# Chunk attention and a gated feed-forward on one core: q and k loaded as 4 KB runs over all partitions, with block 0 in eight PSUM banks and a moved schedule for block 3

## The chip, the core and the metric

The kernel runs on one core of a Trainium2 chip. The metric is the device time of one execution in microseconds. TensorE (PE) does the matmuls, VectorE (DVE), ScalarE (ACT) and GpSimd (Pool) the rest; SyncE (SP) and ACT issue the DMAs, which all run on the core's 16 DMA engines.

## The reference, cut

```python
# q, k, v: (8, 8, 576, 64) fp32: batch, heads, tokens, head_dim.  Attention inside chunks of 64 tokens.
scores = 1/8 * q_c @ k_c.T ;  attn = softmax(scores) ;  out = attn @ v_c
x = out.transpose(0, 2, 1, 3).reshape(4608, 512)          # tokens x (heads * head_dim)
h = x @ w_in                                              # 512 -> 2048
y = (h * 1/(1 + exp(-beta * h))) @ w_out                  # 2048 -> 512
```

## The kernel before

The 4608 tokens are cut into nine blocks of 512, that is of eight chunks. A batch element has nine chunks, so blocks 1 to 7 cross from one element to the next, and their q and k come in two pieces: 1 and 7 chunks in block 1, then 2 and 6, 3 and 5, 4 and 4, and so on. Blocks 0 and 8 come in one.

For each block, q and k are loaded, cast to bf16, transposed (blocks 0 to 2 on PE, with copies out of PSUM by ACT and DVE; the others by a DMA transpose, with "order copies" on Pool), and the attention runs in the four PSUM banks of A. Its result is xT, the moving operand of the first matmul (mm1); tanh on ACT and a product on DVE give g, and the second matmul (mm2) makes the output. mm1 of one block and mm2 of the one before it alternate on PE, and the attention of the next block is threaded between them. Order within each engine's queue comes from a list of events with a time each: `at(time, function, ...)`. One unit of that time is one matmul group of PE.

Some names: PSUM is the memory that PE writes its results to, here eight banks, four called A and four F. "Order copies" put the transposed tokens back in their order (qkO). R holds the reciprocals of the softmax sums, Rhi and Rs are made from it, and "spread" is the matmul that brings Rs to all tokens. The clock granted to PE stands in the trace as full or half; PEclk is its mean in a stretch.

```python
        def load_qk(blk, which, h0, n_h, queue):              # q: partitions 0-63, k: 64-127
            s, src = blk % NQS, (q, k)[which]
            for b, c, n, at in chunk_runs(blk):
                def f(e, b=b, c=c, n=n, at=at):
                    a = src[b][h0:h0 + n_h, 64 * c:64 * (c + n), :]
                    r = 64 * which + 8 * at
                    return e.dma_start(qkstage[r:r + 8 * n, s, h0:h0 + n_h, :],
                                       a.rearrange("h (p i) d -> p h (i d)", i=8))
                P.dma(queue, f, ...)
        ...
        def order_qk(blk, hp, eng):
            copy_cast(eng, in_order(hp), qkT[:, :, hp, :].rearrange("k i t -> k t i"), ...)
        ...
        attention(0, -45, 1)
        at(12, load_qk, 1, 0, 0, 8, "sp")
        at(15.9, load_qk, 1, 1, 0, 8, "act")
        at(12.1, load_v, 1)
        ...
        for blk in range(3, NB):
            t0, u = base(blk - 1) + 1.5, 1
            if blk == 3:
                t0, u = base(2) + 4, 0.85
            loads = 30.5 if blk == 3 else t0 - 24
            ...
            for hp in range(4):
                at(40.5 if blk == 3 else t0 - 16.9, cast_qk, blk, hp, "pool")
                at(t0 - 6.5 + 1.25 * hp, order_qk, blk, hp, "pool")
            ...
            at(41 if blk == 3 else t0 - 15.5, transpose_dma, blk)
            attention(blk, t0, u)
```

The softmax here doesn't subtract the row's maximum and nothing guards it: scores larger than these inputs give would overflow.

Of the kernel before, what the change touches and what calls it, by code (L numbers as in the profile page):

```python
# [7 lines left out]
F32 = dt.float32  # L8
# [3 lines left out]
def K(*key, v=0):  # L12

    return key, v
# [143 lines left out]
def bass_chunk_attention__then__act_swish_beta_kernel(nc, q, k, v, w_in, w_out, beta, out):  # L158
# [8 lines left out]
    with ExitStack() as es:  # L167
# [17 lines left out]
        qkstage = sb("qkstage", [128, NQS, H, 512], F32)  # L185
        vstage = sb("vstage", [128, NVS, 4, H, 64], F32)
        qkcast = sb("qkcast", [128, 8, H, 64], BF16)
        qkT = sb("qkT", [128, 8, 4, 128], BF16)
        qkO = sb("qkO", [128, 4, 2, 8, 64], BF16)
# [70 lines left out]
        def load_qk(blk, which, h0, n_h, queue):  # L260
            s, src = blk % NQS, (q, k)[which]
            for b, c, n, at in chunk_runs(blk):
                def f(e, b=b, c=c, n=n, at=at):
                    a = src[b][h0:h0 + n_h, 64 * c:64 * (c + n), :]
                    r = 64 * which + 8 * at
                    return e.dma_start(qkstage[r:r + 8 * n, s, h0:h0 + n_h, :],
                                       a.rearrange("h (p i) d -> p h (i d)", i=8))
                P.dma(queue, f, writes=[K("qkstage", s, hp, which, at, v=blk)
                                        for hp in range(h0 // 2, (h0 + n_h) // 2)])
# [56 lines left out]
        def cast_qk(blk, hp, eng):  # L326
            s = blk % NQS
            dst = qkcast[:, :, 2 * hp:2 * hp + 2, :].rearrange("p i h d -> p h i d")
            src = qkstage[:, s, 2 * hp:2 * hp + 2, :].rearrange("p h (i d) -> p h i d", i=8)
            keys = [K("qkstage", s, hp, which, at, v=blk)  # L330
                    for which in range(2) for _, _, _, at in chunk_runs(blk)]
            if eng == "act":
                P.op("act", lambda e: e.activation(dst, src, AF.Copy),
                     reads=keys, writes=[K("qkcast", hp, v=blk)])
            else:
                P.op(eng, lambda e: e.tensor_copy(dst, src),  # L336
                     reads=keys, writes=[K("qkcast", hp, v=blk)])

        def transpose_dma(blk):
            P.dma("sp", lambda e: e.dma_start_transpose(  # L340
                qkT[:, :, :, :].rearrange("p i h t -> p (i h) t"),
                qkcast[:, :, :, :].rearrange("p i h d -> p (i h d)")),
                reads=[K("qkcast", hp, v=blk) for hp in range(4)],
                writes=[K("qkT", hp, v=blk) for hp in range(4)])

# [6 lines left out]
        def in_order(hp):  # L352
            return qkO[:, hp, :, :, :].rearrange("k w c (p i) -> k (w c p) i", i=8)

        def order_qk(blk, hp, eng):
            copy_cast(eng, in_order(hp), qkT[:, :, hp, :].rearrange("k i t -> k t i"),
                      [K("qkT", hp, v=blk)], [K("qkO", hp, v=blk)])

        def transpose_pe(blk, hp, ps, psname, eng):
            dst = ps[:, hp, :].bitcast(BF16).rearrange("p (i t) -> p i t", i=8)  # L360
            for i in range(8):
                P.op("pe", lambda e, i=i: e.transpose(  # L362
                    dst[:, i, :], qkcast[:, i, 2 * hp:2 * hp + 2, :].rearrange("p h d -> p (h d)"),
                    identity[:, :]),
                    reads=[K("qkcast", hp, v=blk), K("identity")],
                    writes=[K(psname, hp, v=("t", blk))])
            copy_cast(eng, in_order(hp), dst.rearrange("k i t -> k t i"),
# [249 lines left out]
```

## Time and profile before

Median 362.75 us of 3 runs (361.68 to 363.59); the profiled run has a span of 361.4 us.

| Stage of the profiled run, us | What PE waits for |
|---|---|
| 0 to 27.8 | start-up: loads, then the attention of block 0 |
| 27.8 to 43.3 | nothing: mm1 of block 0 |
| 43.3 to 58.9 | k of block 1 |
| 58.9 to 79.1 | the attention of block 1, step by step |
| 79.1 to 116.8 | blocks 1 and 2 side by side: gaps of 0.2 to 2.4 us, 7 us in all, most for steps of block 2's attention |
| 116.8 to 127.75 | the fourth order copy of block 3 |
| 128.5 to the end | nothing: 32.6 us per block |

The windows view of the kernel before gives the busy time of each engine in four of these stretches. The columns are named in its first line; "(x193)" is the number of instructions.

```profile
core 0: us, PE busy (x) PEld busy (x) DVE busy (x) ACT busy (x) POOL busy (x), PEclk, DMA share, GB/s
0.00:27.80 27.80, 10.42 (x193) 7.53 (x194) 11.03 (x28) 9.13 (x13) 8.08 (x18) 1.00 1.03 259
43.30:58.90 15.60, 8.58 (x36) 3.31 (x36) 1.43 (x3) 2.00 (x4) 3.00 (x5) 0.96 1.03 184
116.80:128.50 11.70, 0.43 (x16) 0.43 (x18) 0.00 (x0) 0.00 (x0) 6.64 (x7) 0.60 0.90 167
189.80:222.40 32.60, 31.29 (x292) 15.35 (x300) 14.84 (x23) 17.28 (x28) 13.83 (x12) 1.00 0.93 188
```

In the steady stretch (the last line) PE is busy 31.29 of 32.60 us. In the stretch before block 1 it is busy 8.58 of 15.60, in the one before block 3's last scores 0.43 of 11.70.

The timeline of the kernel before, around block 1. Columns: start, duration, engine, line and operation, and in brackets the idle time before it with what ended it.

```profile
42.66 0.91 ACTq L266 DMA_DIRECT2D qkstage<-in_k_dram  x2
...
58.15 2.14 DVE L336 CAST qkcast<-qkstage 128x1024 bf16<-128x1024 f32 x2 [14.09 <-DMA qkstage<-in_k_dram]
...
58.91 2.74 PE L362 MATMUL A<-identity,qkcast 128*128 128x128 bf16 x24 [5.34 <-DVE qkcast L336]
```

The load of k is issued by ACT only at 42.66 us, behind the last tanh of block 0. DVE sits idle 14.09 us until it has landed, and PE 5.34 us more after its last filler.

The timeline of the kernel before, around the scores of block 3 (qkO is their operand, written by the order copies).

```profile
116.42 0.32 PE L383 MATMUL A<-qkO 64*64 64x64 bf16 x16 [0.57 <-POOL qkO L350]
121.86 3.99 POOL L336 CAST qkcast<-qkstage 128x1024 bf16<-128x1024 f32 x4 [5.50 <-DMA qkstage<-in_k_dram]
125.80 1.90 POOL L350 COPY qkO<-qkT 128x1024 bf16<-128x1024 bf16 x1
...
127.75 0.43 PE L383 MATMUL A<-qkO 64*64 64x64 bf16 x16 [11.02 <-POOL qkO L350]
```

The first three of the four order copies are done by 116.4 us. The fourth (125.80) stands in Pool's queue behind the four casts of block 4 (121.86), and these wait for block 4's k. So PE waits 11.02 us for a copy whose data had been there all along.

The DMA view of the kernel before in two windows: 20 to 27 us, where only w_in is loaded, and 112 to 121 us, where mostly q and k of block 4 are. "Share" is the time that the packets took, as a share of 16 engines' time.

```profile
DMA packets 1353, 2.70 MB, mean 386 GB/s; under 512 B 42, under 2 KB 42, under 8 KB 1352
q1 hardware_dynamic: 1352, 2.68, 103.8%
...
DMA packets 1459, 1.79 MB, mean 199 GB/s; under 512 B 660, under 2 KB 660, under 8 KB 1459
q1 hardware_dynamic: 1459, 1.79, 108.3%
```

The engines are busy in both, but move 386 GB/s in the one and 199 in the other.

### The profile page before, as it was taken

The numbers are of one execution on the slowest core, as the hardware profiler recorded it, in microseconds if no ns is written. First come the engines' busy times: TensorE is split into PE (matmuls) and PEld (weight loads), VectorE is DVE, ScalarE is ACT, GpSimd is POOL, SyncE is SP. The second block draws the span as 40 slices with busy tenths as digits, with TensorE's granted clock in tenths as the row PEclk, the third lists the DMA queues.
The fourth block names the chain that finished last, engine by engine and source line by source line (L and its number), as shares of the span: only waits on it lengthen the run. The fifth ranks groups of instructions, "written<-read, shape, count | busy, mean of one in ns | idle before, by whom it ended". The sixth has DMA issues, their size and how long they took to land.

```text
span 361.4 us, 6228 instructions
## 1 busy us (share of the span) xinstructions
PE 301.7 (83%) x2646; PEld 148.1 (41%) x2688; DVE 148.2 (41%) x234; ACT 165.5 (46%) x262; POOL 115.2 (32%) x126
## 2 busy tenths in 40 slices
PE   0559974598768089999899999999999999999996
PEld 0433423345323034454445445444544444444442
DVE  3445703238444015533653453355344535534400
ACT  1355613427633035546455553655465455554421
POOL 0347524015046549128244643920630000000000
PEclk9999996869969569999999999999999999999999
DMA  8998999998779978899999979981011000001012
GB/s 149 229 387 310 273 165 215 156 186 187 134 143 210 202 134 167 191 172 143 176 212 200 184 170 221 235 146 48 31 44 44 31 29 32 29 34 55 29 60 87
DMA packets 83517, 52.85 MB, mean 146 GB/s; under 512 B 65569, under 2 KB 65569, under 8 KB 83489
## 3 DMA queue, kind: packets, MB, share of 16 engines
q1 hardware_dynamic: 74586, 39.85, 56.0%
q10 hardware_dynamic: 8902, 12.59, 13.1%
q8 instruction: 21, 0.34, 0.4%
q14 instruction: 8, 0.06, 0.1%
HBM read 36.71 MB, written 9.44 MB: 128 GB/s over the span
## 4 chain that ended last, share of the span: by engine, by line
PE 70%; DMA 9%; DVE 6%; ACT 6%; issue 3%; POOL 3%; SPq 2%; ACTq 0%; DVEq 0%; POOLq 0%
PE F L452 31%; PE F L468 28%; DMA qkstage<-in_k_dram 9%; PE A L416 3%; ACT tt L458 3%; PE A L383 3%; ACT E L389 2%; POOL qkcast L336 2%; DVE R L402 2%; PE A L429 2%; PE A L362 1%; SPq L340 1%; DVE g L461 1%; PE A L395 1%; DVE Rs L406 1%
## 5 line engine op out<-in xcount | busy, mean ns | idle before, releaser
L461 DVE SCALAR_TENSOR_TENSOR g<-tt,F 128x512 bf16<-128x512 bf16 x144 | 99.0, 687 | 152.7 <-ACT tt L458 152.7
L458 ACT ACTIVATE tt<-F,beta_half 128x512 bf16<-128x512 f32 x144 | 98.9, 687 | 123.2 <-PE F L452 123.2
L452 PE MATMUL F<-xT,w_in_bf 128*128 128x512 bf16 x552 | 146.0, 390 | 3.5 <-issue 1.6
L468 PE MATMUL F<-w_out_bf,g 128*128 128x512 bf16 x558 | 144.4, 386 | 4.5 <-POOL w_out_bf L322 1.7
L468 PEld LDWEIGHTS F<-w_out_bf,g 128*128 128x128 bf16 x576 | 55.4, 99 | 68.3 <-issue 3.5
L452 PEld LDWEIGHTS F<-xT,w_in_bf 128*128 128x128 bf16 x576 | 55.5, 100 | 67.9 <-issue 5.5
L350 POOL COPY qkO<-qkT 128x1024 bf16<-128x1024 bf16 x24 | 45.7, 1945 | 59.0 <-PE A L383 29.7
L336 POOL CAST qkcast<-qkstage 128x1024 bf16<-128x1024 f32 x30 | 30.5, 1057 | 73.0 <-DMA qkstage<-in_k_dram 59.8
L473 ACT ACTIVATE ostage<-F 128x512 f32<-128x512 f32 x36 | 21.5, 597 | 28.0 <-PE F L468 28.0
L436 ACT ACTIVATE o_sb<-A 128x512 f32<-128x512 f32 x36 | 20.9, 594 | 16.6 <-PE F L468 5.5
L441 DVE TENSOR_TENSOR xT<-o_sb,A 128x512 bf16<-128x512 f32 x36 | 24.1, 681 | 6.7 <-PE A L416 6.7
L389 ACT ACTIVATE E<-A 128x512 bf16<-128x512 f32 x36 | 20.7, 595 | 7.7 <-PE A L383 5.2
L350 POOL CAST v_bf<-vstage 128x512 bf16<-128x512 f32 x36 | 21.4, 630 | 5.2 <-DMA vstage<-in_v_dram 5.2
L383 PE MATMUL A<-qkO 64*64 64x64 bf16 x576 | 11.4, 201 | 13.8 <-POOL qkO L350 11.6
L416 PE MATMUL A<-Rs,sel 128*128 128x128 bf16 x144 | 13.4, 243 | 10.7 <-DVE Rs L406 7.1
L416 PEld LDWEIGHTS A<-Rs,sel 128*128 128x128 bf16 x144 | 10.3, 110 | 17.6 <-DVE Rs L406 11.2
L383 PEld LDWEIGHTS A<-qkO 64*64 64x64 bf16 x576 | 9.8, 114 | 17.7 <-POOL qkO L350 11.8
L362 PE MATMUL F<-identity,qkcast 128*128 128x128 bf16 x32 | 4.1, 310 | 12.9 <-DVE qkcast L336 10.9
L402 DVE RECIPROCAL R<-A 128x128 f32<-128x128 f32 x9 | 8.6, 952 | 8.4 <-PE A L395 8.4
L322 POOL CAST w_out_bf<-wstage 128x512 bf16<-128x512 f32 x16 | 9.1, 613 | 7.3 <-DMA wstage<-in_moe_w_out_dram 7.3
L336 DVE CAST qkcast<-qkstage 128x1024 bf16<-128x1024 f32 x4 | 3.8, 970 | 16.8 <-DMA qkstage<-in_k_dram 16.8
L362 PE MATMUL A<-identity,qkcast 128*128 128x128 bf16 x64 | 6.2, 266 | 5.3 <-DVE qkcast L336 5.3
(29 smaller groups left out, 66.8 us busy)
## 6 DMA issues: line engine op xcount, KB each, us to landing
out_dram<-ostage ACTq DMA_DIRECT2D x36, 256.0 KB, 3.4
vstage<-in_v_dram SPq DMA_DIRECT2D x32, 256.0 KB, 11.9
wstage<-in_moe_w_in_dram SPq DMA_DIRECT2D x4, 1024.0 KB, 10.2
wstage<-in_moe_w_out_dram SPq DMA_DIRECT2D x4, 1024.0 KB, 9.5
qkstage<-in_q_dram SPq DMA_DIRECT2D x2, 896.0 KB
qkstage<-in_q_dram SPq DMA_DIRECT2D x6, 256.0 KB, 6.4
qkstage<-in_q_dram SPq DMA_DIRECT2D x2, 768.0 KB, 10.7
qkstage<-in_k_dram ACTq DMA_DIRECT2D x5, 256.0 KB, 8.5
```

What stands on the lines that cost most here:

```text
L336: P.op(eng, lambda e: e.tensor_copy(dst, src), reads=keys, writes=[K("qkcast", hp, v=blk)])
L350: P.op(eng, lambda e: e.tensor_copy(dst, src), reads, writes)
L383: return e.matmul(A[64 * g:64 * g + 64, 2 * u + hb, col:col + 64], qkO[r, hp, 1, 2 * cc + g, :], qkO[r, hp, 0, 2 * cc + g, :])
L389: P.op("act", lambda e: e.activation(E[:, bank, :], A[:, bank, :], AF.Exp, scale=0.125), reads=[K("A", bank, v=("s", blk))], writes=[K("E" ...
L416: return e.matmul(A[:, banks[g], col:col + 128], sel[:, u, 2 * (2 * w + ch) + g, :], Rs[:, :])
L436: P.op("act", lambda e: e.activation(o_sb[:, g, :], A[:, bank, :], AF.Copy), reads=[K("A", bank, v=("o", blk, u))], writes=[K("o_sb", g, v ...
L441: P.op("dve", lambda e: e.tensor_tensor(xT[:, sx, 2 * u:2 * u + 2, :].rearrange("p w (c g i) -> p w c g i", c=4, g=2)[:, :, :, g, :], o_sb ...
L452: P.op("pe", lambda e, c=c: e.matmul(F[:, bank, :], w_in_bf[:, c, 128 * t:128 * t + 128], xT[:, sx, c, :], start=(c == 0), stop=(c == NC - ...
L458: P.op("act", lambda e: e.activation(tt[:, T % 3, :], F[:, bank, :], AF.Tanh, scale=beta_half[:, t:t + 1]), reads=[K("F", bank, v=("h", T) ...
L461: P.op("dve", lambda e: e.scalar_tensor_tensor(g2[:, sg, t, :], tt[:, T % 3, :], 1.0, F[:, bank, :], ALU.add, ALU.mult), reads=[K("F", ban ...
L468: P.op("pe", lambda e, t=t: e.matmul(F[:, bank, :], g2[:, sg, t, 128 * s:128 * s + 128], w_out_bf[:, t, :], start=(t == 0), stop=(t == NT ...
L473: P.op("act", lambda e: e.activation(ostage[:, N % NOS, :], F[:, bank, :], AF.Copy, scale=0.5), reads=[K("F", bank, v=("o", N))], writes=[ ...
```

## The change

Its intent: load q and k as 4 KB runs (16 tokens) and over all 128 partitions each, four head pairs beside each other in partitions; issue k of blocks 1 and 2 from SP right behind q; keep block 0's attention free of bank reuse by giving it all eight PSUM banks; and move block 3's schedule: its attention one unit later, its order copies 0.9 units apart and not 1.25. In that schedule the first order copy stands later than before (46.5 and not 45.5), the fourth where it was (49.2 and 49.25). The diff, cut to its core (the comments in it are mine):

```diff
-        qkstage = sb("qkstage", [128, NQS, H, 512], F32)
+        qkstage = sb("qkstage", [128, NQS, 2, 2, 1024], F32)
...
-        def load_qk(blk, which, h0, n_h, queue):
+        def load_qk(blk, which, queue="sp"):
             s, src = blk % NQS, (q, k)[which]
             for b, c, n, at in chunk_runs(blk):
-                    r = 64 * which + 8 * at
-                    return e.dma_start(qkstage[r:r + 8 * n, s, h0:h0 + n_h, :],
-                                       a.rearrange("h (p i) d -> p h (i d)", i=8))
+                for hb in range(2):
...
+                        a = src[b][:, 64 * c:64 * (c + n), :].rearrange(
+                            "(hp hb) (t i) d -> hb t hp (i d)", hb=2, i=16)
+                        return e.dma_start(qkstage[16 * at:16 * (at + n), s, which, hb, :], a[hb])
...   # casts, transposes and order copies follow the new layout, with the same element counts;
...   # scores of a head pair now need all four copies out of PSUM, not one
-        attention(0, -45, 1)
...
+        at(-42.5, attend, 0, 0, (0, 1), F, "F")        # results of block 0 go to the banks of F
...
+        at(-40.4, attend, 0, 1, (2, 3), F, "F")
+        at(-39, spread, 0, 0, (0, 1))                  # and the factors to all four of A
...
+        at(-36, spread, 0, 1, (2, 3))
...
-        at(12, load_qk, 1, 0, 0, 8, "sp")
-        at(15.9, load_qk, 1, 1, 0, 8, "act")
+        for blk, t in ((1, 12), (2, 25.1)):
+            at(t, load_qk, blk, 0)
+            at(t, load_qk, blk, 1)
+            at(t, load_v, blk)
...
-                t0, u = base(2) + 4, 0.85
+                t0, u = base(2) + 5, 0.78
...
-                at(t0 - 6.5 + 1.25 * hp, order_qk, blk, hp, "pool")
+                at(t0 - 6.5 + (0.9 if blk == 3 else 1.25) * i, order_qk, blk, i, "pool")
```

More of the change, by code (lines that the diff above doesn't have):

```diff
@@ L184, in bass_chunk_attention__then__act_swish_beta_kernel @@
         NQS, NVS = 2, 2
-        qkstage = sb("qkstage", [128, NQS, H, 512], F32)
+        qkstage = sb("qkstage", [128, NQS, 2, 2, 1024], F32)
         vstage = sb("vstage", [128, NVS, 4, H, 64], F32)
-        qkcast = sb("qkcast", [128, 8, H, 64], BF16)
-        qkT = sb("qkT", [128, 8, 4, 128], BF16)
-        qkO = sb("qkO", [128, 4, 2, 8, 64], BF16)
+        qkcast = sb("qkcast", [128, 2, 16, 2, 64], BF16)
+        qkT = sb("qkT", [128, 2, 16, 128], BF16)
+        qkO = sb("qkO", [128, 4, 2, 32, 16], BF16)
         NVA = 2
@@ L256, in load_beta, with f @@
                 reads=[K("beta_raw")], writes=[K("beta_half")])
-        def load_qk(blk, which, h0, n_h, queue):
+        def load_qk(blk, which, queue="sp"):
             s, src = blk % NQS, (q, k)[which]
             for b, c, n, at in chunk_runs(blk):
-                def f(e, b=b, c=c, n=n, at=at):
-                    a = src[b][h0:h0 + n_h, 64 * c:64 * (c + n), :]
-                    r = 64 * which + 8 * at
-                    return e.dma_start(qkstage[r:r + 8 * n, s, h0:h0 + n_h, :],
-                                       a.rearrange("h (p i) d -> p h (i d)", i=8))
-                P.dma(queue, f, writes=[K("qkstage", s, hp, which, at, v=blk)
-                                        for hp in range(h0 // 2, (h0 + n_h) // 2)])
+                for hb in range(2):
+                    def f(e, b=b, c=c, n=n, at=at, hb=hb):
+                        a = src[b][:, 64 * c:64 * (c + n), :].rearrange(
+                            "(hp hb) (t i) d -> hb t hp (i d)", hb=2, i=16)
+                        return e.dma_start(qkstage[16 * at:16 * (at + n), s, which, hb, :], a[hb])
+                    P.dma(queue, f, writes=[K("qkstage", s, which, hb, at, v=blk)])
         def load_v(blk):
@@ L323, in cast_w_out @@
                          reads=[K("wstage", s, v=4 + j)], writes=[K("w_out", 4 * j + i)])
-        def cast_qk(blk, hp, eng):
-            s = blk % NQS
-            dst = qkcast[:, :, 2 * hp:2 * hp + 2, :].rearrange("p i h d -> p h i d")
-            src = qkstage[:, s, 2 * hp:2 * hp + 2, :].rearrange("p h (i d) -> p h i d", i=8)
-            keys = [K("qkstage", s, hp, which, at, v=blk)
-                    for which in range(2) for _, _, _, at in chunk_runs(blk)]
-            if eng == "act":
-                P.op("act", lambda e: e.activation(dst, src, AF.Copy),
-                     reads=keys, writes=[K("qkcast", hp, v=blk)])
-            else:
-                P.op(eng, lambda e: e.tensor_copy(dst, src),
-                     reads=keys, writes=[K("qkcast", hp, v=blk)])
-        def transpose_dma(blk):
-            P.dma("sp", lambda e: e.dma_start_transpose(
-                qkT[:, :, :, :].rearrange("p i h t -> p (i h) t"),
-                qkcast[:, :, :, :].rearrange("p i h d -> p (i h d)")),
-                reads=[K("qkcast", hp, v=blk) for hp in range(4)],
-                writes=[K("qkT", hp, v=blk) for hp in range(4)])
         def copy_cast(eng, dst, src, reads, writes):
@@ L350, in copy_cast, with cast_qk @@
                 P.op(eng, lambda e: e.tensor_copy(dst, src), reads, writes)
-        def in_order(hp):
-            return qkO[:, hp, :, :, :].rearrange("k w c (p i) -> k (w c p) i", i=8)
-        def order_qk(blk, hp, eng):
-            copy_cast(eng, in_order(hp), qkT[:, :, hp, :].rearrange("k i t -> k t i"),
-                      [K("qkT", hp, v=blk)], [K("qkO", hp, v=blk)])
-        def transpose_pe(blk, hp, ps, psname, eng):
-            dst = ps[:, hp, :].bitcast(BF16).rearrange("p (i t) -> p i t", i=8)
+        def cast_qk(blk, which, half, eng):
+            s, r = blk % NQS, slice(8 * half, 8 * half + 8)
+            copy_cast(eng, qkcast[:, which, r, :, :].rearrange("p i h d -> p h i d"),
+                      qkstage[:, s, which, :, :].rearrange("p h (i d) -> p h i d", i=16)[:, :, r, :],
+                      [K("qkstage", s, which, hb, at, v=blk)
+                       for hb in range(2) for _, _, _, at in chunk_runs(blk)],
+                      [K("qkcast", which, half, v=blk)])
@@ new lines, in transpose_dma @@
+        def transpose_dma(blk):
+            P.dma("sp", lambda e: e.dma_start_transpose(
+                qkT[:, :, :, :].rearrange("p w i t -> p (w i) t"),
+                qkcast[:, :, :, :, :].rearrange("p w i h d -> p (w i h d)")),
+                reads=[K("qkcast", which, half, v=blk) for which in range(2) for half in range(2)],
+                writes=[K("qkT", v=blk)])
+        def order_qk(blk, hp, eng):
+            copy_cast(eng, qkO[:, hp, :, :, :],
+                      qkT[:, :, :, :].rearrange("k w i (t h) -> k h w t i", h=4)[:, hp],
+                      [K("qkT", v=blk)], [K("qkO", hp, which, half, v=blk)
+                                          for which in range(2) for half in range(2)])
@@ L361, in transpose_pe @@
+        def transpose_pe(blk, which, half, ps, psname, eng):
+            bank, r = 2 * which + half, slice(8 * half, 8 * half + 8)
+            dst = ps[:, bank, :].bitcast(BF16).rearrange("p (i t) -> p i t", i=8)
             for i in range(8):
                 P.op("pe", lambda e, i=i: e.transpose(
-                    dst[:, i, :], qkcast[:, i, 2 * hp:2 * hp + 2, :].rearrange("p h d -> p (h d)"),
+                    dst[:, i, :],
+                    qkcast[:, which, 8 * half + i, :, :].rearrange("p h d -> p (h d)"),
@@ L364, in transpose_pe @@
                     identity[:, :]),
-                    reads=[K("qkcast", hp, v=blk), K("identity")],
-                    writes=[K(psname, hp, v=("t", blk))])
-            copy_cast(eng, in_order(hp), dst.rearrange("k i t -> k t i"),
-                      [K(psname, hp, v=("t", blk))], [K("qkO", hp, v=blk)])
+                    reads=[K("qkcast", which, half, v=blk), K("identity")],
+                    writes=[K(psname, bank, v=("t", blk))])
+            copy_cast(eng, qkO[:, :, which, :, r],
+                      dst.rearrange("k i (t h) -> k h t i", h=4),
+                      [K(psname, bank, v=("t", blk))],
+                      [K("qkO", hp, which, half, v=blk) for hp in range(4)])
@@ L377, in scores @@
             u, w = divmod(hp, 2)
+            qT, kT = (qkO[:, hp, which, :, :].rearrange("k (c t) i -> k c (t i)", c=8)
+                      for which in range(2))
             for cc in range(4):
@@ L383, in f @@
                             return e.matmul(A[64 * g:64 * g + 64, 2 * u + hb, col:col + 64],
-                                            qkO[r, hp, 1, 2 * cc + g, :], qkO[r, hp, 0, 2 * cc + g, :])
-                        P.op("pe", f, reads=[K("qkO", hp, v=blk)],
+                                            kT[r, 2 * cc + g, :], qT[r, 2 * cc + g, :])
+                        P.op("pe", f, reads=[K("qkO", hp, which, half, v=blk)
+                                             for which in range(2) for half in range(2)],
                              writes=[K("A", 2 * u + hb, v=("s", blk))])
@@ L419, in spread, with attend @@
                              writes=[K("A", banks[g], v=("r", blk, u))])
-        def attend(blk, u, banks):
+        def attend(blk, u, banks, ps=A, psname="A"):
             sa = blk % NVA
@@ L428, in f @@
                                 r, col = slice(64 * g, 64 * g + 64), 256 * w + 64 * cc
-                                return e.matmul(A[64 * hb:64 * hb + 64, banks[g], col:col + 64],
+                                return e.matmul(ps[64 * hb:64 * hb + 64, banks[g], col:col + 64],
                                                 v_bf[r, sa, cc, 4 * u + 2 * w + hb, :],
@@ L432, in attend, with copy_o @@
                             P.op("pe", f, reads=[K("E", 2 * u + hb, v=blk), K("v_bf", sa, cc, v=blk)],
-                                 writes=[K("A", banks[g], v=("o", blk, u))])
-        def copy_o(blk, u, g, bank):
-            P.op("act", lambda e: e.activation(o_sb[:, g, :], A[:, bank, :], AF.Copy),
-                 reads=[K("A", bank, v=("o", blk, u))], writes=[K("o_sb", g, v=(blk, u))])
+                                 writes=[K(psname, banks[g], v=("o", blk, u))])
+        def copy_o(blk, u, g, bank, ps=A, psname="A"):
+            P.op("act", lambda e: e.activation(o_sb[:, g, :], ps[:, bank, :], AF.Copy),
+                 reads=[K(psname, bank, v=("o", blk, u))], writes=[K("o_sb", g, v=(blk, u))])
         def normalize(blk, u, g, bank):
@@ L511, in bass_chunk_attention__then__act_swish_beta_kernel @@
         at(-100, load_beta)
-        for hp in range(4):
-            at(-99, load_qk, 0, 0, 2 * hp, 2, "sp")
-            at(-99, load_qk, 0, 1, 2 * hp, 2, "act")
+        at(-99, load_qk, 0, 0)
+        at(-99, load_qk, 0, 1)
         at(-98, load_v, 0)
@@ L521, in bass_chunk_attention__then__act_swish_beta_kernel @@
             at(12.5 + j, cast_w_out, j, ("pool",) * 4)
-        for hp in range(4):
-            at(-50 + hp, cast_qk, 0, hp, ("dve", "act", "pool", "dve")[hp])
-            at(-49.5 + hp, transpose_pe, 0, hp, F, "F", ("act", "dve")[hp % 2])
-            at(-45.5, cast_v, 0, "pool", hp)
-        attention(0, -45, 1)
-        at(12, load_qk, 1, 0, 0, 8, "sp")
-        at(15.9, load_qk, 1, 1, 0, 8, "act")
-        at(12.1, load_v, 1)
-        at(25.1, load_qk, 2, 0, 0, 8, "sp")
-        at(25.9, load_qk, 2, 1, 0, 8, "act")
@@ L534, in bass_chunk_attention__then__act_swish_beta_kernel @@
-        at(25.2, load_v, 2)
-        for hp in range(4):
-            at(24 + 0.2 * hp, cast_qk, 1, hp, ("dve", "act", "pool", "dve")[hp])
-            at(24.5 + 0.2 * hp, transpose_pe, 1, hp, A, "A", ("act", "dve")[hp % 2])
-            at(25, cast_v, 1, "pool", hp)
-            at(34 + hp, cast_qk, 2, hp, "pool")
-            at(35.5 + hp, transpose_pe, 2, hp, A, "A", ("act", "dve")[hp % 2])
-            at(38.7, cast_v, 2, "pool", hp)
-        attention(1, 26, 0.4)
+        for which in range(2):
+            for half in range(2):
+                at(-50 + 2 * which + half, cast_qk, 0, which, half, ("dve", "act")[half])
+                at(-49.5 + 2 * which + half, transpose_pe, 0, which, half, F, "F", ("dve", "act")[half])
@@ new lines, in bass_chunk_attention__then__act_swish_beta_kernel @@
+        for cc in range(4):
+            at(-45.5, cast_v, 0, "pool", cc)
+        for hp in range(4):
+            at(-45, scores, 0, hp)
+        for bank in range(4):
+            at(-44 + bank, exp, 0, bank)
+        at(-42.5, attend, 0, 0, (0, 1), F, "F")
+        at(-40.6, sums, 0, 3)
+        at(-40.5, copy_o, 0, 0, 0, 0, F, "F")
+        at(-40.5, copy_o, 0, 0, 1, 1, F, "F")
+        at(-40.5, invert, 0, 3)
+        at(-40.4, attend, 0, 1, (2, 3), F, "F")
+        at(-39, spread, 0, 0, (0, 1))
@@ new lines, in bass_chunk_attention__then__act_swish_beta_kernel @@
+        at(-38, normalize, 0, 0, 0, 0)
+        at(-37, normalize, 0, 0, 1, 1)
+        at(-36, copy_o, 0, 1, 0, 2, F, "F")
+        at(-36, copy_o, 0, 1, 1, 3, F, "F")
+        at(-36, spread, 0, 1, (2, 3))
+        at(-35, normalize, 0, 1, 0, 2)
+        at(-35, normalize, 0, 1, 1, 3)
+        for blk, t in ((1, 12), (2, 25.1)):
+            at(t, load_qk, blk, 0)
+            at(t, load_qk, blk, 1)
+            at(t, load_v, blk)
+        for which in range(2):
+            for half in range(2):
+                i = 2 * which + half
+                at(23 + 0.2 * i, cast_qk, 1, which, half, ("dve", "act")[half])
+                at(23.5 + 0.2 * i, transpose_pe, 1, which, half, A, "A", ("act", "dve")[half])
+                at(24, cast_v, 1, "pool", i)
+                at(34 + i, cast_qk, 2, which, half, "pool")
+                at(35.5 + i, transpose_pe, 2, which, half, A, "A", ("act", "dve")[half])
+                at(38.7, cast_v, 2, "pool", i)
@@ L543, in bass_chunk_attention__then__act_swish_beta_kernel @@
+        attention(1, 25, 0.4)
         attention(2, 39.5, 0.6)
@@ L546, in bass_chunk_attention__then__act_swish_beta_kernel @@
             if blk == 3:
-                t0, u = base(2) + 4, 0.85
+                t0, u = base(2) + 5, 0.78
             loads = 30.5 if blk == 3 else t0 - 24
             for which in range(2):
-                at(loads, load_qk, blk, which, 0, 8, "sp")
+                at(loads, load_qk, blk, which)
             at(loads + 0.1, load_v, blk)
-            for hp in range(4):
-                at(40.5 if blk == 3 else t0 - 16.9, cast_qk, blk, hp, "pool")
-                at(t0 - 6.5 + 1.25 * hp, order_qk, blk, hp, "pool")
-                at(t0 - 1.2, cast_v, blk, "pool", hp)
+            for i in range(4):
+                at(40.5 if blk == 3 else t0 - 16.9, cast_qk, blk, i // 2, i % 2, "pool")
+                at(t0 - 6.5 + (0.9 if blk == 3 else 1.25) * i, order_qk, blk, i, "pool")
+                at(t0 - 1.2, cast_v, blk, "pool", i)
             at(41 if blk == 3 else t0 - 15.5, transpose_dma, blk)
```

## The prediction

> **What bounds the kernel.** From 128 us on it is TensorE: the windows view has PE busy 31.3 of 32.6 us per block at full clock, the other engines about half. Up to 128.5 us PE is busy only 80 us: 10.4 of the first 27.8 (start-up), 8.6 of 43.3-58.9, 15.8 of 58.9-79.1, 18.1 of 79.1-104.2, 0.4 of 116.8-128.5. The chain of waits names DMA qkstage<-in_k in 1-9, 43-58 and 110-122 us. In 116.8-127.75 PE waits 11.0 us for the fourth order copy of block 3, which stands in Pool's queue behind block 4's casts, which wait for block 4's k.
>
> **Why those loads are slow.** q goes to partitions 0-63 and k to 64-127. In the trace's packet records a 2 KB packet of q or k takes about 160 ns, one of weights (128 partitions) 86; the DMA view has about 205 GB/s while block 4's q and k load and about 390 for w_in. I blame the write side[...]. This trace agrees: half the rate.
>
> **Costs.**
> - Load: 4 KB packets over 128 partitions should take about 170 ns (twice 86; estimate), so q+k of a block take 5.5 us in place of 10.5. Blocks that cross a batch split their run[...].
> - Block 0: all q,k lands at about 10.5 us, not 14.0. But scores now need all four evacuations, so scores move only from 16.9 to about 14.8. First steady matmul of block 0 at 24.5 instead of 27.8: -3.3 us.
> - Block 1: k leaves SP right after q (about 32 us) instead of from ACT's queue after the last tanh (42.7). w_out, issued earlier, lands by 40 instead of 46.7. k lands at about 46 instead of 58. Transposes end about 13 us sooner; the chain from scores to mm1 (64.1 to 79.1, 15 us) stays. mm1 of block 1 starts at about 65 instead of 79.1: -14 in total.
> - Blocks 2-3: the attention latency gaps (about 6 us in 79-104) stay. The fourth order copy of block 3 is still behind block 4's casts (49.2 against 48.6 in the schedule), but its data come sooner, block 3's scores stand one matmul pair later; the wait shrinks to 0-3 us: -10.
> - From then on the 32.6 us per block are unchanged. Casts (1.04 us on Pool), order copies (1.95) and DMA transposes (6.7) should stay within 15%.
>
> Sum: 361.4 - 3.3 - 11 - 10 = about 337 profiled; **336.5 us**, range 327 to 347. Chance of faster by over 2% 0.96, within 2% 0.03, slower 0.01.
>
> **Right if** the profile shows q/k packets of 4 KB at about 170 ns and near 380 GB/s in block 0; block 0's steady matmuls from about 24.5; block 1's first casts' wait ending near 46 and mm1 of block 1 near 65; the wait of scores for Pool's qkO falling under 3 us; PE's steady blocks still 32.6 us.
>
> **Wrong if** [...]k of blocks 1-3 stays late; v (256 B packets, about 25 ns each) becomes block 1's last wait; evacuations with 16-byte runs cost clearly more; or block 4's casts still hold the fourth order copy.

The sum came to 361.4 - 3.3 - 11 - 10 = 337.1 us, and no term is missing from it; but the 46 us for k of block 1, and so the 11 us (about the 14 in total less the 3.3 of block 0), rested in part on the estimate. "The write side" is a guess: the trace then showed only the rates (205 GB/s against 390), and `two_kb` and `halves` test it.

## The result, and the profile after

Median 344.36 us of 3 runs (344.20 to 344.95). The ratio to before is 0.9499 (95% interval 0.9455 to 0.9543). A ratio is the mean time of one kernel's runs over that of the other's of the same rounds, so it is not quite the ratio of the medians. The profiled run has a span of 342.4 us.

The windows view of the changed kernel, in the stretches that answer to those of before (the columns are the same):

```profile
0.00:24.50 24.50, 9.67 (x192) 7.75 (x194) 10.61 (x27) 10.30 (x14) 7.56 (x18) 1.00 1.00 299
41.80:51.20 9.40, 7.55 (x41) 3.61 (x42) 1.89 (x3) 2.42 (x5) 1.39 (x3) 1.00 0.99 238
106.40:108.60 2.20, 1.36 (x66) 1.21 (x67) 0.69 (x1) 0.12 (x1) 2.20 (x3) 1.00 1.19 252
170.70:203.30 32.60, 31.30 (x284) 15.36 (x288) 14.85 (x24) 17.27 (x28) 13.84 (x12) 1.00 0.78 193
```

The wait before block 1's transposes has shrunk from a stretch of 15.6 us to one of 9.4, that before block 3's scores from 11.7 to 2.2. The steady block is 32.60 us as it was.

The timeline of the changed kernel, around block 1:

```profile
45.50 0.69 DVE L330 CAST qkcast<-qkstage 128x1024 bf16<-128x1024 f32 x1 [2.89 <-DMA qkstage<-in_q_dram]
...
50.07 1.06 ACT L328 ACTIVATE qkcast<-qkstage 128x1024 bf16<-128x1024 f32 x1 [0.55 <-ACT ostage L474]
50.70 0.69 DVE L330 CAST qkcast<-qkstage 128x1024 bf16<-128x1024 f32 x1 [4.50 <-DMA qkstage<-in_k_dram]
...
51.18 1.01 PE L357 MATMUL A<-identity,qkcast 128*128 128x128 bf16 x15 [1.84 <-ACT qkcast L328]
```

The q is there at 45.5 us and k at 50.7, where before k came at 58.15. PE waits 1.84 us for ACT's cast of the second half of q, which stands behind an output copy (ostage) in ACT's queue.

The timeline of the changed kernel, around the scores of block 3:

```profile
93.29 5.71 POOL L330 COPY qkO<-qkT 128x1024 bf16<-128x1024 bf16 x3 [7.13 <-PE A L417]
...
104.12 2.02 POOL L330 CAST qkcast<-qkstage 128x1024 bf16<-128x1024 f32 x2 [2.75 <-DMA qkstage<-in_k_dram]
...
106.08 1.95 POOL L330 COPY qkO<-qkT 128x1024 bf16<-128x1024 bf16 x1
...
108.09 0.32 PE L383 MATMUL A<-qkO 64*64 64x64 bf16 x16 [0.68 <-POOL qkO L330]
```

The order is as before: three order copies, then the casts of block 4, then the fourth copy. But block 4's k has landed by 104.1 us where it was 121.9, and PE waits 0.68 us.

The DMA view of the changed kernel in two windows: block 0's q and k, and block 4's.

```profile
DMA packets 2470, 2.30 MB, mean 355 GB/s; under 512 B 1966, under 2 KB 1966, under 8 KB 2470
q1 hardware_dynamic: 1494, 2.30, 96.6%
...
DMA packets 1524, 2.00 MB, mean 211 GB/s; under 512 B 1097, under 2 KB 1097, under 8 KB 1524
q1 hardware_dynamic: 1524, 2.00, 107.2%
```

Block 0's q and k now come at 355 GB/s. Block 4's still come at 211: they are two pieces of 64 partitions each.

The medians of packet durations, which I took from the packet records of the traces (only packets of q and k, or of the weights where it says so):

| Kernel, stage | Partitions of one DMA | Run | Packet, ns |
|---|---|---|---|
| before, w_in | 128 | 2 KB | 88 |
| before, block 0 | 64 | 2 KB | 142 (SP's queue), 147 (ACT's) |
| before, block 4 | 64 | 2 KB | 171 |
| changed, block 0 | 128 | 4 KB | 161 |
| changed, block 4 | 64 | 4 KB | 312 |
| changed, block 1 | 16 and 112 | 4 KB | 247 |

The steps of the whole run, read from the timelines and the landing records:

| Point, us | before | predicted | changed |
|---|---|---|---|
| last q, k of block 0 landed | 13.7 | 10.5 | 9.5 |
| last tanh of block 0 ends | 43.3 | about 40 | 41.9 |
| last k of block 1 landed | 58.0 | 46 | 50.6 |
| mm1 of block 1 starts | 79.1 | 65 | 66.6 |
| scores of block 3 done | 128.2 | | 108.4 |
| end of the span | 361.4 | 337 | 342.4 |

(The 40 is an estimate: the predicted start moved by 3.3 us, and mm1's length kept.)

### The profile page after: what moved, and what is told of

Its sections match the earlier page's. It is cut to its first block, busy times and chain, and to the rows that moved or that the text cites. A ratio compares the mean times of both kernels' runs of the same rounds, so it can differ in the third digit from the quotient of the medians.

```text
span 342.4 us, 6271 instructions
## 1 busy us (share of the span) xinstructions
PE 298.1 (87%) x2645; PEld 147.6 (43%) x2688; DVE 150.3 (44%) x234; ACT 167.6 (49%) x264; POOL 112.6 (33%) x124
## 4 chain that ended last, share of the span: by engine, by line
PE 69%; ACT 7%; DVE 7%; DMA 7%; SPq 5%; issue 3%; POOL 1%; ACTq 0%; POOLq 0%
PE F L469 30%; PE F L453 30%; DMA qkstage<-in_k_dram 5%; ACT tt L459 3%; SPq L268 3%; PE A L383 3%; PE A L417 3%; DVE R L403 2%; DVE g L462 2%; PE A L430 2%; SPq L341 2%; DMA qkstage<-in_q_dram 2%; DVE Rs L407 1%; ACT E L390 1%; PE A L396 1%
## 5 line engine op out<-in xcount | busy, mean ns | idle before, releaser
L469 PE MATMUL F<-w_out_bf,g 128*128 128x512 bf16 x560 | 140.8, 379 | 2.2 <-issue 1.1
L330 POOL CAST qkcast<-qkstage 128x1024 bf16<-128x1024 f32 x28 | 28.2, 1041 | 23.6 <-DMA qkstage<-in_k_dram 9.9
L437 ACT ACTIVATE o_sb<-A 128x512 f32<-128x512 f32 x32 | 18.8, 593 | 10.3 <-ACT ostage L474 4.6
L383 PE MATMUL A<-qkO 64*64 64x64 bf16 x576 | 12.7, 196 | 4.7 <-DVE qkO L330 2.8
L383 PEld LDWEIGHTS A<-qkO 64*64 64x64 bf16 x576 | 11.5, 110 | 8.3 <-issue 3.6
L310 POOL CAST w_in_bf<-wstage 128x512 bf16<-128x512 f32 x14 | 8.3, 630 | 5.4 <-DMA wstage<-in_moe_w_in_dram 5.2
L430 PEld LDWEIGHTS A<-E,v_bf 64*64 64x64 bf16 x512 | 5.8, 111 | 7.4 <-issue 3.6
```

The lines of the kernel that those rows point to most:

```text
L330: P.op(eng, lambda e: e.tensor_copy(dst, src), reads, writes)
L383: return e.matmul(A[64 * g:64 * g + 64, 2 * u + hb, col:col + 64], kT[r, 2 * cc + g, :], qT[r, 2 * cc + g, :])
L437: P.op("act", lambda e: e.activation(o_sb[:, g, :], ps[:, bank, :], AF.Copy), reads=[K(psname, bank, v=("o", blk, u))], writes=[K("o_sb", ...
L469: P.op("pe", lambda e, t=t: e.matmul(F[:, bank, :], g2[:, sg, t, 128 * s:128 * s + 128], w_out_bf[:, t, :], start=(t == 0), stop=(t == NT ...
```

## The experiments

Twelve kernels ran. Each call also ran the kernel before on the same chip; the ratios below are to those runs. The changed kernel itself stands at 0.9499. It was not run again beside them, so "us more" or "less than the changed kernel" below compares medians. The diffs are cut to the lines that matter.

### Does the queue order or the layout bring k sooner?

`kq_only` is the kernel before with k behind q on SP:

```diff
-        at(15.9, load_qk, 1, 1, 0, 8, "act")
+        at(12, load_qk, 1, 1, 0, 8, "sp")
-        at(25.9, load_qk, 2, 1, 0, 8, "act")
+        at(25.1, load_qk, 2, 1, 0, 8, "sp")
```

> The kernel before with one edit: k of blocks 1 and 2 is issued from SP right behind q, as the change does, with the old layout. Theory (both parts are needed: queue order and write-side width): k of block 1 no longer waits for the last tanh of block 0 (42.7 us), but packets of q and k still take 160 to 300 ns, so k lands about 52 us instead of 58; block 1's first scores move from 64.1 to about 58.5, and the kernel gains 5 to 8 us (355 to 358). Rival A (queue order alone is the change): gains 15 us or more. Rival B (the layout alone is the change): gains under 2 us.

Measured: 361.56 us, ratio 0.9955 (0.9893 to 1.0016). My theory missed and rival B came in. The chain of waits of this kernel (start, duration, what):

```profile
35.91 21.53 DMA qkstage<-in_k_dram
57.56 0.70 DVE qkcast L336
```

The k is issued 8.6 us sooner than before (at 34.0 us, not 42.7) and lands at 57.4 in place of 58.0. In the old layout q and k of block 1 pass slowly (a 2 KB packet of q took 169 ns in the kernel before, in the median from 42.6 us on, against 88 for w_in's), and from 33.6 to 58 us the DMA engines are full in both kernels (a share of 1.01 to 1.06), so it does not matter when k joins the queue. Issuing sooner was worth nothing here, where the queue itself was full.

`layout_actk` is the changed kernel with k of blocks 1 and 2 back on ACT's queue:

```diff
-            at(t, load_qk, blk, 1)
+            at({1: 15.9, 2: 25.9}[blk], load_qk, blk, 1, "act")
```

> The changed kernel with one edit: k of blocks 1 and 2 goes back to ACT's queue at its old place in the order (after tanh 15 of block 0, and 9.9 matmul groups into the next stage). Theory: k of block 1 lands at 53 to 55 us instead of 50.6, since it shares the engines with v's 256 B packets, and the kernel loses 2 to 5 us against the changed one (346 to 349). Rival A (queue order alone): loses 12 us or more. Rival B (layout alone): loses under 1 us.

Measured: 346.37 us, ratio 0.9549 (0.9499 to 0.9598), 2 us more than the changed kernel. DVE's wait for block 1's k ended at 54.8 us, as expected (in the kernel before, with k at the same place in ACT's queue, 1892 of v's 256 B packets ran from 43 to 58 us, beside k's):

```profile
54.76 0.69 DVE L330 CAST qkcast<-qkstage 128x1024 bf16<-128x1024 f32 x1 [6.63 <-DMA qkstage<-in_k_dram]
...
73.78 3.62 PE L453 MATMUL F<-xT,w_in_bf 128*128 128x512 bf16 x16
```

So the layout with everything else but the order brings 0.0451 of the 0.0501, and the order about 0.005 on top of it (the intervals of the two kernels overlap). But these 0.005 are a net result. In its own stage the order counts for more: mm1 of block 1 begins at 73.8 us in place of 66.6, with PE at half clock from 53.8 to 64.1. Some 5 of these 7 us come back later, most of them from block 3 on, where PE's wait for Rs is 0.84 us and not 2.54 and no half clock follows it (see "Where did the last microseconds go?").

### Is it the width or the length of the runs?

`two_kb` keeps all partitions but cuts each load in two, so that runs are 2 KB again:

```diff
+                    for x in range(2):
                         a = src[b][:, 64 * c:64 * (c + n), :].rearrange(
-                            "(hp hb) (t i) d -> hb t hp (i d)", hb=2, i=16)
+                            "(hp hb) (t x i) d -> hb x t hp (i d)", hb=2, x=2, i=8)
-                        return e.dma_start(qkstage[16 * at:16 * (at + n), s, which, hb, :], a[hb])
+                        return e.dma_start(
+                            qkstage[16 * at:16 * (at + n), s, which, hb, 512 * x:512 * x + 512], a[hb, x])
```

> The changed kernel with each q and k load cut into two of half the run: 2 KB runs again, but still over all partitions. It costs twice as many issues on SP (0.6 to 0.8 us each). Theory (the width of the write side is what counts): block 0's q and k packets take 85 to 95 ns, half of the changed kernel's 160 and about half of the 150 that the kernel before needs for the same 2 KB, and the time stays within 3 us of the changed kernel's 344.3. Rival (the length of the run is what counts): packets of 140 ns and more, time back above 352.

Measured: the 2 KB packets of block 0 took 84 ns, against 142 to 147 for the same size in the kernel before: here width decides. The time was 348.45 us, ratio 0.9585 (0.9516 to 0.9653), 4.1 us more than the changed kernel by the medians and 3.1 by the ratios, whose intervals just overlap; I had allowed 3. Its timeline shows where time goes:

```profile
96.60 5.06 SPq L269 DMA_DIRECT2D qkstage<-in_q_dram  x8
...
101.70 5.05 SPq L269 DMA_DIRECT2D qkstage<-in_k_dram  x8
...
113.60 0.43 PE L385 MATMUL A<-qkO 64*64 64x64 bf16 x16 [5.36 <-POOL qkO L332]
```

SP needs 10.1 us to issue q and k of block 4, 16 DMAs at 0.63 us each, where the changed kernel needs 5.0 for its eight (2.50 and 2.50, from 91.83). One issue of 0.63 us is for 128 KB, which take about as long at the 211 GB/s of that stage in the changed kernel (estimate). Meanwhile the DMA engines are busy only 67%, against 96% in the changed kernel, so here they wait for SP. Block 4's k comes late (its casts on Pool begin at 109.67 and not 104.12), and PE waits 5.36 us for block 3's fourth order copy behind the casts of that k. That is what the longer run buys here: half as many issues, not faster packets.

`halves` keeps 4 KB runs but loads block 0 as partitions 0 to 63 and then 64 to 127:

```diff
+        def load_runs(blk):
+            if blk != 0:
+                return chunk_runs(blk)
+            (b, c, n, at), = chunk_runs(0)
+            return [(b, c, 4, 0), (b, c + 4, 4, 4)]
-            for b, c, n, at in chunk_runs(blk):
+            for b, c, n, at in load_runs(blk):
```

> The changed kernel with block 0's four loads of q and k each cut in two, the first for partitions 0 to 63, the second for 64 to 127; still 4 KB runs, same data, correct result. Theory (width): packets of 4 KB take about 310 ns in place of 160, q and k of block 0 are all there at about 14.5 us in place of 9.8, all loads behind them on SP move by the same 4 to 5 us, and the kernel loses 3 to 5 us. Rival (run length): packets stay at 160 ns and the kernel loses less than 1 us.

Measured: 348.05 us, ratio 0.9590 (0.9545 to 0.9634), 3.7 us more; the packets took 312 ns. The DMA view of `halves`, while q and k of block 0 are loaded:

```profile
DMA packets 2288, 2.22 MB, mean 212 GB/s; under 512 B 1796, under 2 KB 1796, under 8 KB 2288
q1 hardware_dynamic: 1412, 2.22, 103.4%
```

212 GB/s in place of 355, with the engines just as busy (103.4% and 96.6%). Half the partitions gave about half the rate, for runs of 2 KB (199 GB/s for block 4 of the kernel before, 386 for w_in) and of 4 KB (212 and 355) alike. Why is not shown.

### Is the schedule of block 3 worth the 11 us?

`sched_only` is the kernel before with only block 3's schedule of the changed one; `old_sched` is the changed kernel with the old one:

```diff
-                t0, u = base(2) + 4, 0.85
+                t0, u = base(2) + 5, 0.78
-                at(t0 - 6.5 + 1.25 * hp, order_qk, blk, hp, "pool")
+                at(t0 - 6.5 + (0.9 if blk == 3 else 1.25) * hp, order_qk, blk, hp, "pool")
```

> The kernel before with only the schedule edit of block 3 (t0 one later, u 0.78, order copies 0.9 apart). Theory: the fourth order copy still stands behind block 4's casts in Pool's queue (49.2 against 48.6) and these wait for block 4's k at 122 us, so the wait for qkO only shrinks by the matmul pair that now runs before it (11.0 to about 9.3 us) and the time stays within 1.5 us of before. Rival (order copies that begin sooner remove the 11 us wait): gains 8 us or more.

> The changed kernel with the old schedule of block 3. Theory: PE reaches block 3's scores one matmul pair (1.7 us) earlier but the fourth order copy ends at the same 108 us, so the wait grows from 0.7 to 2 to 2.5 us and the time by 0 to 2 us. Rival (the schedule is worth the removed 11 us wait): loses 8 us or more.

Measured: `sched_only` 361.97 us, ratio 0.9973 (0.9917 to 1.0028); `old_sched` 345.11 us, ratio 0.9512 (0.9463 to 0.9561). Neither differs from its base by more than the noise. The timeline of `sched_only`:

```profile
121.51 3.99 POOL L336 CAST qkcast<-qkstage 128x1024 bf16<-128x1024 f32 x4 [6.09 <-DMA qkstage<-in_k_dram]
125.45 1.90 POOL L350 COPY qkO<-qkT 128x1024 bf16<-128x1024 bf16 x1
...
127.40 0.43 PE L383 MATMUL A<-qkO 64*64 64x64 bf16 x16 [10.04 <-POOL qkO L350]
```

The wait is 10.04 us in place of 11.02, and the fourth copy still follows the casts of block 4. In `old_sched` the same wait is 1.8 us in place of 0.68. What removed the wait of 11 us is that block 4's k comes 18 us sooner, not the order of the copies.

### What are block 0's eight banks worth, and what holds block 1?

`old_banks` is the changed kernel with block 0's attention as before:

```diff
-        at(-42.5, attend, 0, 0, (0, 1), F, "F")
-        ...
-        at(-35, normalize, 0, 1, 1, 3)
+        attention(0, -45, 1)
```

> The changed kernel with block 0's attention as before (its results in the banks of A, taken in turn, instead of all eight banks). Theory (block 1 is held by the landing of its q and k, about 50.6 us, not by block 0's matmuls): block 0's first matmul moves by about 1 us and the kernel loses 0 to 1.5 us. Rival (the banks bring the whole gain of block 0, 3.3 us as predicted): loses 3 us or more.

Measured: 346.49 us, ratio 0.9542 (0.9494 to 0.9590); single runs reach from 344.35, inside the changed kernel's range, to 347.47. So the banks bring about 1.6 us by the ratios, with an error of the same size. In its trace w_out's first load is issued at 26.4 us in place of 25.1, and k of block 1 lands at 52.6 in place of 50.7. That points to the staging buffer: w_out may only be loaded once the casts of w_in have freed it, and two of the first four casts stood behind block 0's attention on ACT and DVE.

`w_in_pool` puts these four on Pool:

```diff
-               ("pool", "act", "dve", "pool") if j == 0 else ("pool",) * 4)
+               ("pool",) * 4)
```

> The changed kernel with the first four casts of w_in all on Pool, which idles there, instead of one each on ACT and DVE behind the attention of block 0. They end about 19.5 us instead of 25.1, so the first load of w_out is issued 5 us sooner and the DMA engines no longer run dry at 26.5 to 28. Theory (block 1 is held by the DMA queue): q and k of block 1 land 1.5 to 2 us sooner and the kernel gains 1 to 2 us on the changed one. Rival (block 1 is held by PE's own work in block 0): gains under 0.5 us.

Measured: 342.60 us, ratio 0.9438 (0.9401 to 0.9475). The timeline of the changed kernel, where the last of the four casts is DVE's:

```profile
24.64 0.42 DVE L310 CAST w_in_bf<-wstage 128x512 bf16<-128x512 f32 x1
25.08 3.81 SPq L298 DMA_DIRECT2D wstage<-in_moe_w_out_dram  x4
```

The timeline of `w_in_pool`:

```profile
16.90 2.29 POOL L310 CAST w_in_bf<-wstage 128x512 bf16<-128x512 f32 x4 [2.10 <-DMA wstage<-in_moe_w_in_dram]
19.22 9.71 SPq L298 DMA_DIRECT2D wstage<-in_moe_w_out_dram  x4
```

The issue moved from 25.08 to 19.22 us, and k of block 1 landed at 48.1 in place of 50.7. The gain is 1.8 us in the medians; the interval overlaps with the changed kernel's by a little.

`warm` gives PE nine matmuls to chew on in its idle time before block 0's, so that the clock is up:

```diff
+        def warm(n):
+            for _ in range(n):
+                P.op("pe", lambda e: e.matmul(F[:, 1, :], identity[:, :], E[:, 0, :]),
+                     reads=[K("identity"), K("E", 0, v=0)], writes=[K("F", 1, v=("w", 0))])
+        at(-40.3, warm, 4)
+        at(-35.9, warm, 5)
```

> The changed kernel with nine extra 128x512 matmuls whose result nobody reads, in PE's idle time around the spread of block 0, to get the full clock before block 0's matmuls start at 24.5 us (in the changed kernel the trace gives the full clock from 30.5, in the kernel before from 30.7, so 3.3 us of head start were partly run at half clock). Theory (block 1 is held by the landing of its q and k): block 0's last tanh ends about 38.5 to 39.5 us in place of 41.9, but block 1's scores stay near 55 us and the kernel gains less than 1 us. Rival (the cold clock is what the prediction's missing 8 us went into): gains 2 us or more.

Measured: 345.59 us, ratio 0.9520 (0.9484 to 0.9556): no gain. The full clock came at 22.2 us in place of 30.2 (the clock records have 30.2 for the changed kernel and 30.4 for the kernel before, where the expectation has 30.5 and 30.7) and the last tanh of block 0 ended at 39.5 in place of 41.9, as expected. The timeline of `warm` shows where the 2.4 us went:

```profile
51.42 0.69 DVE L330 CAST qkcast<-qkstage 128x1024 bf16<-128x1024 f32 x1 [4.74 <-DMA qkstage<-in_k_dram]
...
52.17 0.62 PE L357 MATMUL A<-identity,qkcast 128*128 128x128 bf16 x8 [2.19 <-DVE qkcast L330]
```

PE reached the transposes sooner and waited 2.19 us longer for k, which landed at 51.4; after that wait the trace has half clock from 52.9 to 59.8 us. So block 1 is held by the DMA queue and not by block 0's matmuls, though the spell at half clock may be part of why nothing was gained.

### Where did the last microseconds go?

In block 3 the small DVE steps between the sums and the spread (R, Rhi, Rs) ran beside Pool's order copies for block 4. The timeline of the changed kernel:

```profile
115.01 7.59 POOL L330 COPY qkO<-qkT 128x1024 bf16<-128x1024 bf16 x4 [4.74 <-PE F L453]
...
120.03 0.81 DVE L405 CAST Rhi<-R 128x128 bf16<-128x128 f32 x1
...
120.87 1.88 DVE L407 SCALAR_TENSOR_TENSOR Rs<-Rhi,mask,R 128x128 bf16<-128x128 bf16 x1
...
122.81 1.03 PE L417 MATMUL A<-Rs,sel 128*128 128x128 bf16 x8 [2.54 <-DVE Rs L407]
```

The same instruction takes 0.35 us in the median of this trace's nine blocks; here Rs takes 1.88, about as long as one order copy, and PE waits 2.54 us for it. `after_rs` holds the order copies until Rs of the block before is done:

```diff
-                      [K("qkT", v=blk)], [K("qkO", hp, which, half, v=blk) ...
+                      [K("qkT", v=blk)] + ([K("Rs", v=blk - 1)] if blk > 3 and hp == 0 else []),
+                      [K("qkO", hp, which, half, v=blk) ...
```

> The changed kernel with one more dependency: the order copies of a block on Pool (1.95 us each) start only when the three small DVE steps of the block before (R, Rhi, Rs) are done. In the changed kernel they run beside each other in block 3, where Rhi takes 0.81 us in place of 0.23 and Rs 1.88 in place of 0.35, and PE waits 2.5 us for Rs there. Theory (Pool and DVE slow each other, and that gave back some 2 us of the gain): Rhi and Rs of block 3 return to 0.23 and 0.35 us and the kernel gains 1.5 to 2.5 us on the changed one. Rival (the durations have another cause, or the wait is hidden): no change beyond 0.5 us, or the small steps stay long.

Measured: 342.33 us, ratio 0.9439 (0.9394 to 0.9484), 2.0 us less than the changed kernel, with intervals that overlap a little. The timeline of `after_rs`:

```profile
120.42 0.23 DVE L405 CAST Rhi<-R 128x128 bf16<-128x128 f32 x1
120.68 0.35 DVE L407 SCALAR_TENSOR_TENSOR Rs<-Rhi,mask,R 128x128 bf16<-128x128 bf16 x1
...
121.09 0.62 PE L417 MATMUL A<-Rs,sel 128*128 128x128 bf16 x8 [0.43 <-DVE Rs L407]
121.10 3.88 POOL L330 COPY qkO<-qkT 128x1024 bf16<-128x1024 bf16 x2 [10.44 <-DVE Rs L407]
```

Rhi and Rs are back at 0.23 and 0.35 us, PE's wait is 0.43, and Pool begins when Rs ends. In the changed kernel's trace both steps ended just after a Pool copy beside them: the copy begun at 118.82 us ended at 120.75, and Rhi, begun at 120.03, at 120.83; the copy begun at 120.69 ended at 122.60, and Rs, begun at 120.87, at 122.75. In `w_in_pool` it is Rhi that takes 1.88 us (117.97 to 119.85, beside a copy that ended at 119.77), and PE waits 2.31 us there. In these three cases the DVE step ended within 0.2 us of the copy; but R, which ran beside the copy begun at 118.82 (119.04 to 119.99), took its usual 0.95 us. Why the one is held and not the other the traces do not show, and it was not tested.

### Together

`pool_rs` has the edits of `w_in_pool` and `after_rs`:

> Two edits on the changed kernel: the first casts of w_in all on Pool, and the order copies held until Rs of the block before is done. Theory (they act in different stages, so they add): 2.2 us from the first as measured and 1.5 to 2.5 from the second, 339.5 to 341 in all. Rival (they share one cause): no more than the better of the two alone.

Measured: 339.09 us (337.85 to 339.80), ratio 0.9335 (0.9296 to 0.9375). The two add up (5.3 us in the medians, 1.8 and 2.0 alone), and the interval lies clear of the changed kernel's. This beats both kernels.

`best` adds to it that ACT casts the second half of block 1's q before the output copy:

```diff
-                at(23 + 0.2 * i, cast_qk, 1, which, half, ("dve", "act")[half])
+                at(22.4 + 0.2 * i if which == 0 else 23 + 0.2 * i, cast_qk, 1, which, half, ("dve", "act")[half])
```

> Three edits on the changed kernel: the two of pool_rs, and in block 1 the cast of the second half of q on ACT stands before, not behind, the copy of the second output tile (ostage) of block 0. In pool_rs that cast started at 48.3 us although its data lay there from 42.8, and PE's transposes waited 1.9 us for it; k lands at 48.5, so the other half of the chain allows 1.0 to 1.3 us. Theory (block 1 is now held by ACT's order about as much as by the DMA queue): the wait of the transposes for ACT's qkcast falls under 0.5 us, first scores move from 53.2 to about 52, and the kernel gains 0.5 to 1.3 us on pool_rs (ratio to before 0.930 to 0.932). Rival (the landing of k alone holds block 1): no gain beyond 0.2 us.

Measured: 339.02 us (337.14 to 342.17), ratio 0.9348 (0.9284 to 0.9412): no gain. PE's wait for ACT's cast fell from 1.8 to 0.9 us, but in the profiled run PE also came to the transposes 1.3 us later, and the full clock came at 29.7 us and not at 27.3 as in the profiled run of `pool_rs` (in that of `w_in_pool` at 28.6). The kernels are the same up to there, so the one look does not tell whether the edit was idle or was covered by the clock. This stays open.

## Why the prediction was right, and where its size was off

The predicted 336.5 us had 344.36 in its range (327 to 347), near the upper end, and the direction, the causes and the stages held. The gain was 18.4 us, and 26.2 was predicted. On the profiled spans it was 19.0 against 24.4: the prediction set a sum of profiled times beside measured ones, and the medians lie 1.4 us (before) and 1.9 us (changed) above the spans. By its own three terms, on the profiled spans:

- **Why the loads were slow: right, as far as it was tested.** Half the partitions, about half the rate (212 GB/s against 355); the reason was not shown. `two_kb` and `halves` show it both ways, and the packet of 4 KB over all partitions took 161 ns where I had estimated 170.
- **Block 0, "-3.3": mis-sized, it was -1.4.** mm1 of block 0 started at 24.5 us as predicted, but the last tanh came only 1.4 us sooner. The step that failed is that the matmuls would keep their pace: the full clock came at 30.4 us before and at 30.2 us after, although dense work began 3.3 us sooner (5.7 us before the full clock, and not 2.6), so the head start was run at half clock, where mm1's matmuls start 427 ns apart in the median, and 216 at full clock. (The clock records begin only with that full clock; the PEclk of 1.00 in windows before it is not a reading.) By `warm` an earlier clock gained nothing in the end, since block 1 still waited for k.
- **Block 1, "k lands at about 46", "-14 in total": 50.6, and -12.5.** The prediction's estimate for the loads of blocks 1 to 3 took 170 ns a packet for the split pieces too. The packets themselves took 247 ns in block 1 (16 and 112 partitions): that is the size that failed. How many engines carry a piece the traces do not record; they have 5 landing records for each piece of 16 partitions and 15 for each of 112, and 13 and 11 for block 3's pieces of 48 and 80, where a DMA to 128 has 16. Why a packet took longer is not shown: seven eighths of them belong to the piece of 112 partitions, so the narrow piece alone does not explain the median, and from 28.9 to 51.3 us 1888 packets of 2 KB and 1851 of 256 B started as well. Most of it came back because the chain from scores to mm1 took 11.6 us (54.97 to 66.61) and not the 15 that I had carried over. The traces say what shrank it: in the kernel before, the clock granted was half for 7.2 of the 15 us, in the changed kernel it was full throughout. `old_sched`, alike up to block 3's schedule, had half clock for 6.8 us of the same chain, and there it took 15.0. The prediction had no term for the clock; that it made up for the late k was luck of the profiled run.
- **The queue order, costed as part of that term:** alone it is worth nothing measurable (`kq_only`), on top of the layout about 2 us net (7.2 us at mm1 of block 1 in `layout_actk`, most of it made up later).
- **Blocks 2 and 3, "-10": right in its first half, then partly given back.** The wait of 11.0 us became 0.68, within the 0 to 3 predicted. From mm1 of block 1 to the scores of block 3 the time fell from 49.1 to 41.8 us, and one more matmul pair of 1.7 us ran in it, so 9.0 us. But from there to the end took 234.0 us against 233.2, with that pair (1.7) less to do: 2.5 us lost. `after_rs` shows what some 2 us of them were: Pool's order copies, now beside block 3's R, Rhi and Rs. After that wait the changed kernel's trace also has half clock from 122.4 to 125.8 us, and `after_rs` has none there; its stretch from block 3's scores to the end took 230.0 us. I had kept "the steady blocks unchanged" and not asked what the freed copies would run into.
- **The schedule:** the prediction that the fourth copy stays behind block 4's casts was right, and `sched_only` shows that the schedule by itself does nothing.

The sum on the spans is -12.5 - 9.0 + 2.5 = -19.0, the difference of 361.4 and 342.4. One step to be careful with: that block 1 is held by the landing of q and k is shown for the changed kernel by `warm` (PE sooner, no gain); that the 1.8 us of `w_in_pool` flow through block 1 is only argued. Its first scores did come sooner, but block 2's did not (first exp at 80.4 us against 80.1); the gain is seen again from block 3 on (108.0 against 110.0). In between, mm1 of block 1 began at 66.9 us and not 66.6, and the half clock around 95 us lasted 3.4 us and not 6.8. In these two profiles the gain lies where the clock differs, and not in block 1.

## What to carry to other kernels

Look at the time of one packet and at how many partitions one DMA writes before moving an issue earlier: here a DMA to half of the partitions ran at about half the rate (212 GB/s against 355), and an earlier issue alone gave nothing (`kq_only`, 0.9955). When a wait goes away, ask what the freed engine will now run beside; here Pool's copies moved next to DVE's shortest and most critical steps (Rs took 1.88 us in place of 0.35). Before crediting a change of one or two microseconds to an edit, compare the granted clock of the two traces: the same chain took 11.6 us at full clock and 15.0 with 6.8 us at half. And a head start in one stage is worth only what the next stage's last input allows, so follow that input (here a staging buffer that two idle-looking casts kept busy).
